# Two pieces of GpSimd's work placed behind a block's sums: sketched attention followed by an exact-GELU MLP

## Chip, cores and metric

The kernel runs on one core of a Trainium2 chip. The metric is device time in microseconds; times given are medians over runs, and a separate profiled execution gives the trace. The engines are called TensorE (PE in the profile; PEld is its weight load), VectorE (DVE), ScalarE (ACT), GpSimd (POOL) and SyncE (SP, which here only issues transfers).

## What is computed

Attention with a polynomial sketch in place of the softmax, and behind it an MLP of two matmuls with an exact GELU between them:

```python
def phi(x):                                   # S1, S2: 8 x 32
    a = np.einsum('rd,bhsd->bhsr', S1, x)
    b = np.einsum('rd,bhsd->bhsr', S2, x)
    return np.einsum('bhsi,bhsj->bhsij', a, b).reshape(*x.shape[:-1], 64)
q_p, k_p = phi(q), phi(k)                     # q, k, v: 4 x 4 x 1088 x 32
kv = np.einsum('bhsf,bhsd->bhfd', k_p, v)
z = np.sum(k_p, axis=2)
num = np.einsum('bhsf,bhfd->bhsd', q_p, kv)
den = np.einsum('bhsf,bhf->bhs', q_p, z)[..., None] + 1e-06
x = (num / den).transpose(0, 2, 1, 3).reshape(4352, 128)
h = x @ w_in                                  # 128 x 2048
out = (0.5 * h * (1 + erf(h / sqrt(2)))) @ w_out   # 2048 x 128
```

w_in, w_out, S1 and S2 come as 64-bit floats, so the kernel forms 32-bit floats from their words on the chip.

## The kernel before

**Tiling.** The 1088 tokens of each of the four batches are two chunks of 512 and a remainder of 64. The eight chunks of 512 are n = 0 to 7, and the remainders of all batches together are the last one. For each chunk the 2048 hidden channels are 16 tiles of 128, so a step t is one pair of a chunk and a hidden tile. Steps 0 to 3 are tiles 0 to 3 of chunk 0, steps 4 to 11 tiles 0 to 7 of chunk 1, steps 12 to 23 the rest of chunk 0, steps 24 to 31 the rest of chunk 1, and from step 32 on each chunk has its 16 steps in a row.

**Order.** Each engine executes its instructions in the order of the text: the last lines of the kernel tie every instruction to the one before it on its engine. The text is the loop at L1289. In each step it first issues the hidden tile's matmul and GELU (`hidden`, L770 and L777), then, in every fourth step, the sums of the block that this tile completes (`token_sums`), then the entries that `at(t, function, arguments)` put in the list of that step, in the order in which they were entered, then stores and then products on TensorE that are due. So the step and the place in the list set where a piece of work stands in an engine's queue.

**The second matmul.** The first tiles of chunks 0 and 1 (4 and 8 of them) are multiplied by w_out as usual (`project`, L955). All others go in blocks of four hidden tiles, by a scheme with seven products in place of eight. A block needs sums of its activations, which GpSimd makes in `token_sums` (L821 to L824; they are called bits_low, bits_a, bits_e and bits_m in the profile, after the buffers that they share with the rounding), and sums of quarters of w_out, which GpSimd makes once for each piece of w_out in `channel_sums` (L808 to L811, into tiles called small). w_in and w_out are each five pieces: 0 to 4. The products are issued by `two_products` (L856) some steps behind the block's last tile. The blocks in question are, in chunk 0, the first (its last tile is step 15), the second (step 19) and the third (step 23); the second uses piece 3 of w_out and the third piece 4.

**Rounding.** Pieces 2 to 4 of w_in and w_out are formed in steps 4 to 13 by VectorE and ScalarE, in the order of the list `turns`. On VectorE, `end` issues the mantissa (L302), the sign (L307) and the product (L312). For `turns[4]`, which is piece 4 of w_in, GpSimd does the product: `multiply`, in step 12.

**The keys of the second batch (batch 1).** In steps 13 to 18 VectorE turns and multiplies its keys (L383, L1082 to L1104) and the next queries (L556), and in step 24 TensorE sums keys and values (`z_sum`, `kv_and_attend`, both by way of L456), after which VectorE folds z (L511 to L514) for TensorE's sketch of the queries (L606). For the 64 remaining tokens the values lie in `v_rem_aug`, a tile that GpSimd clears (L364) and into which it copies the 64 rows (L366) that a transfer brought; this is `widen_v_rem(1)`. The transfer is one of many that SyncE issues in a row.

**GpSimd's queue from step 12 to 23**: `widen_v_rem(1)`, `multiply` of w_in's piece 4, `channel_sums(2)` (step 13), the sums of the first block (step 15), `channel_sums(3)` (16), `channel_sums(4)` (18), the sums of the second block (19) and those of the third (23).

Of the kernel before, what the change touches and what calls it, by code (L numbers as in the profile page):

```python
# [16 lines left out]
def kernel(  # L17
# [1046 lines left out]
    def at(t, f, *a):  # L1064
        slots[t].append(lambda: f(*a))
# [112 lines left out]
    for k, acts in enumerate(schedule):  # L1178
# [4 lines left out]
            at(t, by_scalar, turns[k], *what)  # L1183
        if k + 1 < len(turns):
            at(t1, end, turns[k])
    at(12, widen_v_rem, 1)
    at(12, multiply, turns[4])
    for i, t in ((1, 5), (0, 6), (2, 13)):
        at(t, channel_sums, i)
    at(16, channel_sums, 3)  # L1190
# [6 lines left out]
    at(17, features_rem, 1)  # L1197
    at(17, add_tokens, 1)
    at(18, query_turn, 2)
    at(18, channel_sums, 4)  # L1200

    at(24, z_sum, 1)
    at(24, fold_z, 1)
# [181 lines left out]
```

## Time and profile before

| | |
|---|---|
| time before | 257.99 us median of 3 runs (257.95 to 258.36) |
| profiled execution | 259.27 us, its span 257.5 us |
| TensorE clock granted | 0.999 |
| busy in the span | TensorE 252.0, VectorE 159.5, ScalarE 113.6, GpSimd 176.8 us |
| read from HBM, written | 10.88 MB, 2.23 MB |

The span is the stretch from the first to the last instruction of the trace, and all places in the trace are counted in us from its start. The profiled execution is one single run with the profiler on; its own time, not the median, belongs to its span. In a row of the timeline the bracket gives the idle time of the engine ahead of the instruction, and what ended it. Such a releaser is inferred from semaphore events.

### The profile page before, as it was taken

Reading aid. Unit: us, or ns where it says so; the run is one execution under the profiler, and the core shown is the slowest. Engines: PE = TensorE matmul, PEld = TensorE weight load, DVE = VectorE, ACT = ScalarE, POOL = GpSimd, SP = SyncE. Lnnn points to the kernel's source line nnn. Section 1 sums busy time; section 2 is a strip of 40 time slices with the busy share of each in tenths; the row PEclk is TensorE's granted clock in tenths of the full one; section 3 lists DMA queues with packets and bytes.
Section 4 is the critical chain, followed back from the end, with each engine's and each line's share of the span. In section 5 each row is a group of like instructions: output and inputs, shape, how many; then the busy total and the mean of one; then the engine's idle time right before and its main releaser. Section 6 shows DMA issues by size and latency. Waiting matters only on the chain.

```text
span 257.5 us, 5987 instructions
## 1 busy us (share of the span) xinstructions
PE 252.0 (98%) x2421; PEld 131.2 (51%) x2421; DVE 159.5 (62%) x334; ACT 113.6 (44%) x219; POOL 176.8 (69%) x193
## 2 busy tenths in 40 slices
PE   8999999989999999999999999999999999999995
PEld 4744444455444545544444455455544444445784
DVE  4899999929799997590187986399407000700282
ACT  3783885323626333443335332533435333532541
POOL 3517219998858778487758775687758777877950
PEclk9999999999999999999999999999999999999999
DMA  6789538821000101102000002000110200020021
GB/s 209 209 257 305 147 71 222 210 64 15 0 3 12 29 4 19 25 1 42 0 3 0 0 7 38 1 4 0 26 17 3 42 0 3 4 36 3 0 35 32
DMA packets 29083, 13.50 MB, mean 52 GB/s; under 512 B 21888, under 2 KB 27264, under 8 KB 29056
## 3 DMA queue, kind: packets, MB, share of 16 engines
q1 hardware_dynamic: 28624, 12.79, 20.5%
q8 instruction: 19, 0.31, 0.6%
q10 hardware_dynamic: 432, 0.33, 0.4%
q14 instruction: 8, 0.07, 0.1%
HBM read 10.88 MB, written 2.23 MB: 51 GB/s over the span
## 4 chain that ended last, share of the span: by engine, by line
PE 81%; DMA 6%; POOL 6%; SPq 4%; ACT 1%; issue 1%; DVE 0%; POOLq 0%
PE h_ps L770 38%; PE o_ps L856 33%; DMA block<-in_moe_w_out_dram 6%; PE w_ps L926 2%; SPq L125 2%; PE w_ps L456 1%; PE w_ps L606 1%; PE w_ps L661 1%; PE w_ps L987 1%; POOL bits_low L821 1%; DMA v_rem<-in_v_dram 1%; SPq L181 1%; PE o_ps L952 1%; POOL small L811 1%; POOL bits_m L824 0%
## 5 line engine op out<-in xcount | busy, mean ns | idle before, releaser
L770 PE MATMUL h_ps<-xT,w_in 128*64 128x512 f32 (+2 forms) x536 | 137.9, 567 | 0.0
L777 ACT ACTIVATE block<-h_ps 128x512 f32<-128x512 f32 (+1 forms) x132 | 75.4, 572 | 121.1 <-PE h_ps L770 119.1
L856 PE MATMUL o_ps<-block,w_out 128*64 128x256 f32 x232 | 59.5, 379 | 0.0
L821 POOL TENSOR_TENSOR bits_low<-block 128x512 f32<-128x512 f32 x29 | 38.0, 1311 | 28.9 <-ACT block L777 28.9
L770 PEld LDWEIGHTS h_ps<-xT,w_in 128*64 128x64 f32 (+1 forms) x536 | 41.4, 140 | 27.1 <-issue 8.2
L856 PEld LDWEIGHTS o_ps<-block,w_out 128*64 128x64 f32 x232 | 31.7, 137 | 38.6 <-issue 27.7
L822 POOL TENSOR_TENSOR bits_a<-block 128x512 f32<-128x512 f32 x29 | 37.0, 1277 | 12.3 <-ACT block L777 12.3
L871 DVE COPY sums<-o_ps 64x256 f32<-64x256 f32 x8 | 3.3, 416 | 60.2 <-PE o_ps L856 60.2
L823 POOL TENSOR_TENSOR bits_e<-bits_a,block 128x512 f32<-128x512 f32 x29 | 37.3, 1288 | 2.3
L824 POOL TENSOR_TENSOR bits_m<-block,bits_e 128x512 f32<-128x512 f32 x29 | 37.0, 1277 | 2.3
L856 PE MATMUL o_ps<-bits_low,small 128*64 128x256 f32 x116 | 29.9, 380 | 1.3 <-POOL bits_low L821 1.3
L856 PE MATMUL o_ps<-block,small 128*64 128x256 f32 x116 | 30.0, 380 | 0.0
L856 PE MATMUL o_ps<-bits_m,w_out 128*64 128x256 f32 x116 | 29.8, 379 | 0.0
L856 PE MATMUL o_ps<-bits_a,small 128*64 128x256 f32 x116 | 29.8, 379 | 0.0
L856 PEld LDWEIGHTS o_ps<-block,small 128*64 128x64 f32 x116 | 15.6, 137 | 18.5 <-issue 11.1
L856 PE MATMUL o_ps<-bits_e,small 128*64 128x256 f32 x116 | 17.7, 383 | 0.0
L856 PEld LDWEIGHTS o_ps<-bits_low,small 128*64 128x64 f32 x116 | 15.6, 137 | 1.9 <-POOL bits_low L821 1.8
L856 PEld LDWEIGHTS o_ps<-bits_a,small 128*64 128x64 f32 x116 | 15.8, 137 | 0.5 <-POOL bits_a L822 0.3
L856 PEld LDWEIGHTS o_ps<-bits_m,w_out 128*64 128x64 f32 x116 | 15.9, 137 | 0.0
L618 DVE STREAM_TRANSPOSE w_ps<-w_ps 128x512 f32<-128x512 f32 (+1 forms) x7 | 4.8, 687 | 17.1 <-ACT xT L672 12.7
L856 PEld LDWEIGHTS o_ps<-bits_e,small 128*64 128x64 f32 x116 | 7.8, 136 | 11.5 <-issue 9.0
L955 PE MATMUL o_ps<-g,w_out 128*128 128x512 f32 x24 | 12.1, 600 | 0.1
(221 smaller groups left out, 317.7 us busy)
## 6 DMA issues: line engine op xcount, KB each, us to landing
block<-in_moe_w_in_dram SPq DMA_DIRECT2D x3, 512.0 KB, 13.0
block<-in_moe_w_out_dram SPq DMA_DIRECT2D x3, 512.0 KB, 12.8
k<-in_k_dram SPq DMA_DIRECT2D x12, 128.0 KB, 2.8
v<-in_v_dram SPq DMA_DIRECT2D x12, 128.0 KB, 2.8
q<-in_q_dram SPq DMA_DIRECT2D x24, 64.0 KB, 2.4
out_dram<-oT SPq DMA_DIRECT2D x21, 64.0 KB, 2.3
q_first<-in_q_dram SPq DMA_DIRECT2D x2, 256.0 KB, 3.9
v<-in_v_dram SPq DMA_DIRECT2D x2, 256.0 KB, 4.2
```

The costliest lines, as they stand in the source:

```text
L125: sp.dma_start(out=q_sb[n][h * 32:(h + 1) * 32].rearrange("t x j d -> t (x j d)"), in_=q[n // NCH, h, at:at + CW, :].rearrange("(t n) d -> ...
L618: dve.transpose(out=tok, in_=ps[:, :, :H2])
L770: pe.matmul(ps[rows, :W], lhsT=w[:, rows], rhs=xT[n][:, :W], start=True, stop=True)
L777: act.activation(out=g_of[n, fi][:, :W], in_=ps[:, :W], func=ACT.Gelu)
L821: pool.tensor_sub(out=s[3], in0=a11, in1=a21)
L822: pool.tensor_add(out=s[1], in0=a21, in1=a22)
L823: pool.tensor_sub(out=s[2], in0=s[1], in1=a11)
L824: pool.tensor_sub(out=s[4], in0=a12, in1=s[2])
L856: pe.matmul(acc[n][bank][half * 64:(half + 1) * 64, col:col + HW], lhsT=fixed, rhs=moving, start=opens and e == 0 and name in "4715", stop ...
L871: dve.tensor_copy(out=N[lo, 0, one], in_=a0[lo, one])
L926: pe.matmul(acc[NMAIN][rows, COLS_REM[name]], lhsT=tokens[:, rows], rhs=fixed, start=k == 0 and name == ORDER_REM[0], stop=k == BLOCKED // ...
L955: pe.matmul(o_of[n][:, cols], lhsT=w_tile(w_out_sb, fi), rhs=g[:, cols], start=first, stop=final)
```

## The change

Two entries of the list go to other steps. `widen_v_rem(1)` goes from step 12, where it stood ahead of `multiply`, to step 15, where it follows the sums of the first block. `channel_sums(4)` goes from step 18 to step 19, where it follows the sums of the second block. No instruction is added or left out.

```diff
-    at(12, widen_v_rem, 1)
     at(12, multiply, turns[4])
+    at(15, widen_v_rem, 1)
     for i, t in ((1, 5), (0, 6), (2, 13)):
         at(t, channel_sums, i)
     at(16, channel_sums, 3)
...
     at(18, query_turn, 2)
-    at(18, channel_sums, 4)
+    at(19, channel_sums, 4)
```

GpSimd's queue after it: `multiply` (step 12), `channel_sums(2)` (13), the sums of the first block and `widen_v_rem(1)` (15), `channel_sums(3)` (16), the sums of the second block and `channel_sums(4)` (19), the sums of the third block (23).

## The prediction

> **What bounds the kernel now.** The page's busy times come first: TensorE is busy for 252.0 of 257.5 us.
>
> ```profile
> PE 252.0 (98%) x2421; PEld 131.2 (51%) x2421; DVE 159.5 (62%) x334; ACT 113.6 (44%) x219; POOL 176.8 (69%) x193
> ```
>
> So a gain can only come from the few places where TensorE stands still. The view of waits (engine, line, releaser: us in total, times, longest us) shows one wait of TensorE's matmuls on GpSimd, and one long wait of GpSimd on a transfer:
>
> ```profile
> POOL v_rem_aug L366 <- DMA v_rem<-in_v_dram: 10.5, 1, 10.5
> ...
> PE o_ps L856 <- POOL bits_low L821: 1.3, 1, 1.3
> ```
>
> The chain that ended last, in order of time, joins the two (start us, us, what):
>
> ```profile
> 35.23 2.30 DMA v_rem<-in_v_dram
> ...
> 37.65 0.75 POOL v_rem_aug L366
> 38.40 1.26 POOL w_in L312
> ...
> 50.50 0.46 POOL small L811
> 50.95 1.24 POOL bits_low L821
> 52.19 0.04 issue
> 52.23 0.86 PE o_ps L856 x5
> ...
> 55.89 1.25 PE w_ps L456 x80
> ```
>
> The transfer of the remainder's values lands at 37.53. GpSimd then copies it (L366), multiplies w_in's last piece (L312), and works without a pause until the first of the second block's sums (bits_low, L821) ends at 52.19. From 52.23 on the chain is TensorE alone but for the output's last step. Both things that the change moves lie in that run.
>
> The stall's true size is read from the timeline (start us, us, instruction), against an undisturbed stretch with the same order (two steps of products and hidden matmuls, then L456):
>
> ```profile
> 50.30 0.59 PE L856 MATMUL o_ps<-block,small 128*64 128x256 f32 x2
> 52.23 0.43 PE L856 MATMUL o_ps<-bits_low,small 128*64 128x256 f32 x1 [1.33 <-POOL bits_low L821]
> ...
> 55.82 0.32 PE L456 MATMUL w_ps<-k_s,ones 128*32 128x64 f32 x8
> ...
> 94.14 0.38 PE L856 MATMUL o_ps<-block,small 128*64 128x256 f32 x1
> ...
> 97.68 0.32 PE L456 MATMUL w_ps<-k_s,ones 128*32 128x64 f32 x8
> ```
>
> Undisturbed it takes 97.68 - 94.14 = 3.54 us from these products to L456; here 55.82 - 50.30 = 5.52. The stall costs 1.98 us, more than the 1.33 in its row, because the products that don't need bits_low ran ahead and stood idle after. Ahead of 50.30 and behind 55.82 I see no other stall that GpSimd causes and TensorE pays for.
>
> **The copy (step 12 to 15).** L364 and L366 leave the place ahead of L312. The cleared tile needs no data, but the copy holds all that is behind it in GpSimd's queue until 37.53. L312 then waits only for VectorE's sign step of the same piece, which ends at 35.77 + 0.68 = 36.45:
>
> ```profile
> 35.77 0.68 DVE L307 SCALAR_TENSOR_TENSOR bits_e<-block,bits_r 128x512 uint32<-128x512 uint32 x1
> ...
> 38.17 3.27 DVE L307 SCALAR_TENSOR_TENSOR bits_e<-block,bits_r 128x512 uint32<-128x512 uint32 x1
> 40.97 0.79 POOL L811 TENSOR_TENSOR small<-w_out,small 128x128 f32<-128x128 f32 x1
> 41.72 1.72 POOL L821 TENSOR_TENSOR bits_low<-block 128x512 f32<-128x512 f32 x1
> ...
> 88.02 0.20 POOL L364 MEMSET v_rem_aug<- 128x128 f32 x1
> 88.29 0.29 POOL L366 COPY v_rem_aug<-v_rem 64x128 f32<-64x128 f32 x1
> ```
>
> With the 0.04 us that a release takes here (52.19 to 52.23) L312 starts at 36.49 in place of 38.36: 1.87 us sooner. Its input and the channel sums behind it are ready by then (w_out's piece 2 was written by 29.4). The first block's bits_low needs the GELU of step 14 (37.83 + 0.62 = 38.45), its second sum that of step 15 (39.45 + 0.60 = 40.05); GpSimd reaches them at 36.49 + 1.25 + 1.82 = 39.6 and 40.8, so neither wait shows. The clearing and the copy come back behind the block's four sums, on the path now: 0.56 us by the later rows above (88.02 to 88.58), 0.48 + 0.75 = 1.23 by the rows at 26.70 and 37.65. I take 0.56, since the 0.75 met VectorE's L302 and the reduction that VectorE runs at 46 shows no such effect on the sums beside it. The transfer has then long landed. Who needs the copy is kv_sum at 56.85 - 1.98 = 54.9; it is ready before 47.
>
> **The channel sums of the last piece (step 18 to 19).** They took 49.13 to 50.91, 1.78 us, directly ahead of bits_low of the second block; that goes. They come behind that block's sums: their first reader is the third block's products at 61.00 - 1.98 = 59.0.
>
> **The sum.** L312's start to the end of bits_low was 52.19 - 38.36 = 13.83. Less 1.78, plus 0.56: 12.61 (13.28 with the dear copy). Started at 36.49 it ends at 49.10 (49.77). One thing is added: VectorE's last rounding (L302, L307, L312) falls on the same stretch. Before, two of its three steps held GpSimd up, L811 by 0.34 and L821 by 0.44 us against their sister rows, which is in the 13.83; now L302 (37.60) falls on it too. I take one more such delay, 0.45: 49.55, at the worst 50.22. Below, if fewer collide than before, 48.3. The second block's GELUs are done by 45.52. TensorE wants bits_low at 50.30. **The stall goes whole, 1.98 us, with 0.08 to 2 us to spare.**
>
> What is late next: the second block's next sum, bits_a, ends 1.24 us behind bits_low, at 50.8 (51.5 at the worst), and is wanted two steps of 0.86 behind 50.30, at 52.0; its last sum ends 3.87 us behind, at 53.4, and is wanted at 59.06 - 1.98 = 57.1; the last channel sums at 55.2, wanted at 59.0; the third block's bits_low at 56.5, wanted at 59.0, its last sum at 60.4, wanted at 65.73 - 1.98 = 63.75. On VectorE, k_s (L1104) ends at 50.95 and L456 wants it at 53.84; L556 ends at 52.16 and z's step (L511) would start at 54.23. All hold. Behind them the whole order follows TensorE, and no load is outstanding past 62 us that is wanted soon, so 1.98 us reach the end.
>
> The Trainium skill (SBUF — State Buffer, Who interferes with whom) states that a VectorE instruction with two SBUF inputs and a GpSimd one that reads SBUF exclude each other, the later one blocked until the first finishes. The trace agrees that they collide, but the 3.27 row ran across four GpSimd instructions, not one. By the page each of the three steps would get in after one instruction and hold GpSimd for its own 0.68 us: estimated from rows, 3 x 0.68 - 0.78 = 1.26 in place of 0.45, bits_low at 50.36, and a loss of 0.06 us.
>
> **The time.** Profiled execution 259.27 us (span 257.5 and 1.77 around it): 259.27 - 1.98 = 257.29. The median of the runs shown, 257.99, lies 1.28 lower; on it I forecast **256.0 us**. Repeated runs lie within 257.95 to 258.36, so about 0.2% (0.52 us) can be told from no change.
>
> **Rivals.**
> (a) GpSimd is still late in part: all three VectorE steps hold it for their whole 0.68 us and the copy costs 1.23: 36.49 + 13.28 + 1.26 = 51.03, a stall of 0.73, time 256.7. For it: the collisions at 38 to 43. Against: no GpSimd row there lost over 0.46.
> (b) VectorE is late. GpSimd now runs from 36.49 with gaps only where an instruction needs the one before it (the 0.07 us ahead of L811, and between the later sums). If each rounding step waits for a gap of its own: 39.0, 42.4, 44.3, the rounding ends at 44.9 in place of 42.30, 2.6 us late; L556 then ends at 54.8, 0.5 past 54.23, and TensorE's sketches wait some 0.4 us: time 256.4.
> (c) Slower: the same mechanism, but VectorE is let in only when the first block's sums and the copy are over, at about 45.2. Three steps of 0.65 end at 47.1, 4.8 late; 2.1 of it is covered, so TensorE stands 2.7 us at the sketches ahead of L606 and the time is 257.99 - 1.98 + 2.7 = 258.7. It turns slower from a lateness of about 4.1 us. Against: the 3.27 row was let in at the gap of 40.90.
> (d) No change: the stall returns at the second block's next sum or at the third block. Against: the margins above of 1.2 us and more (0.5 at the worst). 258.0.
>
> **Chances.** Forecast 0.76 (255.7 to 256.3), (a) 0.06, (b) 0.06, (c) 0.07, (d) 0.05. (a) and (b) are still faster by over 0.2%: faster 0.88, same 0.05, slower 0.07. The range takes in the forecast's spread and (a) and (b): 255.5 to 256.9.
>
> **What would show it.** In the changed profile: L312 on GpSimd near 36.5; the wait of 10.5 us under L366 gone; L366 at about 45 to 46 and about 0.3 us long; bits_low of the second block ending at 48.3 to 50.2; no row of L856 waiting on bits_low; L456 near 53.8 with nothing ahead of it; the chain on TensorE all through that stretch. I am wrong if L312 on VectorE ends past 44.5, if L511 starts later than 0.4 us behind L456, or if bits_low ends past 50.3.

## The result and the profile after

The changed kernel takes 257.75 us (median of 22 runs, 257.29 to 258.15). The kernel before, run beside it, takes 258.57 us (22 runs, 257.95 to 259.94). The ratio is 0.9968, with a 95% interval of 0.9957 to 0.9978: faster by 0.82 us, 0.3%, where 2.0 us were forecast. The 256.0 us of the forecast lie below every run of the changed kernel.

The profiled execution of the changed kernel took 257.70 us, its span 255.9. First the page: TensorE's busy time, and the chain that ended last, by engine.

```profile
PE 251.6 (98%) x2421; PEld 131.2 (51%) x2421; DVE 157.5 (62%) x334; ACT 113.6 (44%) x219; POOL 177.3 (69%) x193
...
PE 98%; ACT 0%; DVE 0%; issue 0%
```

In the kernel before, transfers (6%), GpSimd (6%) and SyncE's queue (4%) held about a sixth of that chain, which went back from the stall through GpSimd's wait to the loads ahead of it; now it is TensorE from end to end. The timeline of the place in question, GpSimd first and TensorE second (start us, us, instruction, and in brackets what the engine waited for):

```profile
36.91 1.31 POOL L312 TENSOR_TENSOR w_in<-bits_m,bits_e 128x512 f32<-128x512 f32 x1 [9.71 <-DVE bits_e L307]
38.16 0.92 POOL L808 TENSOR_TENSOR small<-w_out 128x128 f32<-128x128 f32 x1
...
46.74 0.29 POOL L366 COPY v_rem_aug<-v_rem 64x128 f32<-64x128 f32 x1
...
48.77 1.28 POOL L821 TENSOR_TENSOR bits_low<-block 128x512 f32<-128x512 f32 x1
```

```profile
50.73 0.38 PE L856 MATMUL o_ps<-block,small 128*64 128x256 f32 x1
50.74 0.38 PE L856 MATMUL o_ps<-bits_low,small 128*64 128x256 f32 x1
...
54.27 0.32 PE L456 MATMUL w_ps<-k_s,ones 128*32 128x64 f32 x8
```

GpSimd's product (L312) waits for VectorE alone, the copy takes 0.29 us behind the first block's sums, and bits_low of the second block ends at 50.05, ahead of the products that read it. These now take 54.27 - 50.73 = 3.54 us to L456, the undisturbed figure to the hundredth. The stall is gone whole. So the question is why a stall of 1.98 us that went whole brought 0.82.

Two differences between the two profiles point to the answer. The first products of the second block begin at 50.73 now and began at 50.30 then. Of these 0.43 us, 0.38 are there already ahead of the place where the copy stood: VectorE's sign step (L307), for which GpSimd's product waits, ends at 36.83 now and ended at 36.45 then. And SyncE issued the three transfers among which is the one that the copy waits for from 31.67 on in this execution, from 35.23 on in the one before. Nothing in the order of SyncE's queue was changed, so this may vary from one execution to the next.

**Theory A**: the profiled execution of before was not a usual one. The values land usually before VectorE releases L312, so that L312 starts late only in a few executions, and the stall is usually some 0.6 to 0.7 us; what causes it there is the channel sums ahead of bits_low. **Theory B**: the landing delays GpSimd in a usual execution too, the stall is near 2 us, and the change has a cost of about 1.1 us elsewhere.

### The profile page after: what moved, and what is told of

It reads as the page before. It is cut to its first block, busy times and chain, and to the rows that moved or that the text cites. A ratio compares the mean times of both kernels' runs of the same rounds, so it can differ in the third digit from the quotient of the medians.

```text
span 255.9 us, 5988 instructions
## 1 busy us (share of the span) xinstructions
PE 251.6 (98%) x2421; PEld 131.2 (51%) x2421; DVE 157.5 (62%) x334; ACT 113.6 (44%) x219; POOL 177.3 (69%) x193
## 4 chain that ended last, share of the span: by engine, by line
PE 98%; ACT 0%; DVE 0%; issue 0%
PE h_ps L770 45%; PE o_ps L856 35%; PE o_ps L955 4%; PE w_ps L926 2%; PE w_ps L456 1%; PE w_ps L606 1%; PE w_ps L661 1%; PE w_ps L987 1%; PE w_ps L572 1%; PE h_ps L786 1%; PE o_ps L952 1%; PE h_ps L348 1%; PE o_ps L445 1%; PE w_ps L1074 1%; PE w_ps L681 0%; PE o_ps L397 0%
## 5 line engine op out<-in xcount | busy, mean ns | idle before, releaser
L821 POOL TENSOR_TENSOR bits_low<-block 128x512 f32<-128x512 f32 x29 | 37.5, 1292 | 28.2 <-ACT block L777 28.2
L770 PEld LDWEIGHTS h_ps<-xT,w_in 128*64 128x64 f32 (+1 forms) x536 | 40.8, 140 | 27.1 <-issue 8.2
L822 POOL TENSOR_TENSOR bits_a<-block 128x512 f32<-128x512 f32 x29 | 37.1, 1280 | 11.6 <-ACT block L777 11.5
L823 POOL TENSOR_TENSOR bits_e<-bits_a,block 128x512 f32<-128x512 f32 x29 | 37.4, 1289 | 2.3
L856 PEld LDWEIGHTS o_ps<-bits_e,small 128*64 128x64 f32 x116 | 7.9, 137 | 11.5 <-issue 9.1
## 6 DMA issues: line engine op xcount, KB each, us to landing
q_first<-in_q_dram SPq DMA_DIRECT2D x2, 256.0 KB, 3.9
v<-in_v_dram SPq DMA_DIRECT2D x2, 256.0 KB, 4.1
```

The source lines that it names most:

```text
L770: pe.matmul(ps[rows, :W], lhsT=w[:, rows], rhs=xT[n][:, :W], start=True, stop=True)
L821: pool.tensor_sub(out=s[3], in0=a11, in1=a21)
L822: pool.tensor_add(out=s[1], in0=a21, in1=a22)
L823: pool.tensor_sub(out=s[2], in0=s[1], in1=a11)
L856: pe.matmul(acc[n][bank][half * 64:(half + 1) * 64, col:col + HW], lhsT=fixed, rhs=moving, start=opens and e == 0 and name in "4715", stop ...
```

## The experiments

In all of them the comparison is with the kernel before, run on the same chip.

### The halves of the change, an early transfer, and the change again

The copy alone:

```diff
-    at(12, widen_v_rem, 1)
     at(12, multiply, turns[4])
+    at(15, widen_v_rem, 1)
```

> Only the copy is moved (step 12 to 15); the channel sums of the last piece stay ahead of the second block's sums. Theory A (in a usual execution the remainder's values land early, so that GpSimd's w_in product waits for VectorE in the kernel before too; what makes bits_low of the second block late is the work ahead of it): in the profile after, bits_low ended at 50.05 and was wanted at 50.73; 1.78 us of channel sums put it at 51.83, 1.1 us late, a stall of about 1.2, and a time 1.2 us above the changed kernel's, that is 0.4 us ABOVE the kernel before. Theory B (the landing holds the w_in product up in a usual execution too, so the move is worth 1.3 us at the path, and the change carries a cost of about 1.1 us elsewhere): 0.2 to 1.3 us BELOW the kernel before.

Measured: 258.96 us (11 runs) against 258.55, ratio 1.0019 (1.0010 to 1.0029): slower by 0.4 us, as theory A had it to a tenth. TensorE's timeline has a stall of 55.68 - 50.98 - 3.54 = 1.16 us:

```profile
50.98 0.59 PE L856 MATMUL o_ps<-block,small 128*64 128x256 f32 x2
52.09 0.43 PE L856 MATMUL o_ps<-bits_low,small 128*64 128x256 f32 x1 [0.52 <-POOL bits_low L821]
...
55.68 0.32 PE L456 MATMUL w_ps<-k_s,ones 128*32 128x64 f32 x8
```

The half that takes the 10.5 us wait out of the view of waits makes the kernel slower: GpSimd's product now waits 9.72 us for VectorE in its place, and the copy, which stood in idle time, stands on the path.

The channel sums alone:

```diff
-    at(18, channel_sums, 4)
+    at(19, channel_sums, 4)
```

> Only the channel sums of the last piece are moved (step 18 to 19); the copy stays ahead of the w_in product. Theory A: no stall in a usual execution, since 1.78 us go and at most 0.6 were late; the time is the changed kernel's within 0.1 us, 0.8 us below the kernel before. A late landing (37.5) would leave a stall of about 0.1 to 0.2 only. Theory B: 1.78 of the 1.98 us go here, less a hidden cost if this half carries it: anything from 0.7 to 1.8 us below the kernel before, and slower than the changed kernel by 0.1 to 0.3.

Measured: 257.57 us (9 runs), ratio 0.9971 (0.9961 to 0.9982), against 257.69 for the whole change in the same comparison; the ratios of the two, 0.9971 and 0.9968, can't be told apart. This half brings all of the gain. In its profile the values land early, bits_low ends at 48.02 + 1.27 = 49.29, and the products take 54.12 - 50.58 = 3.54 us to L456:

```profile
48.02 1.27 POOL L821 TENSOR_TENSOR bits_low<-block 128x512 f32<-128x512 f32 x1
...
50.58 0.38 PE L856 MATMUL o_ps<-block,small 128*64 128x256 f32 x1
...
54.12 0.32 PE L456 MATMUL w_ps<-k_s,ones 128*32 128x64 f32 x8
```

A gain of this size was also within theory B's range, so this run doesn't decide between the two.

The order as before, with the transfer ahead of the loads of batch 1:

```diff
+        load_rem("v", 1)
         for b in range(1, B):
             load_keys(b)
...
-                for n, b1 in (("k", 1), ("k", 3), ("v", 1), ("v", 2), ("v", 3)):
+                for n, b1 in (("k", 1), ("k", 3), ("v", 2), ("v", 3)):
```

> The order on GpSimd as before; only the transfer of the remainder's second values is issued ahead of the keys and values of batch 1, some 6 us sooner, so that the copy finds them there. Theory A: nothing changes in the usual execution: a stall of 0.6 to 0.7 us remains, bits_low of the second block ends about 0.6 us past the time it is wanted, L312 on GpSimd starts on VectorE's L307; the median is 0 to 0.2 us below the kernel before, with fewer high times. Theory B: L312 starts 1.9 us sooner, the stall goes nearly whole: 1.5 to 1.9 us below the kernel before.

Measured: 258.33 us (12 runs, 257.99 to 258.90), ratio 0.9996 (0.9986 to 1.0006): no difference that can be told. The transfer was issued at 15.22, 15 to 21 us sooner than in the profiles that leave it in its place, and not the 6 us of the expectation, so the landing is out of the way altogether (line numbers are one higher in this kernel), and yet:

```profile
27.42 0.35 POOL L367 COPY v_rem_aug<-v_rem 64x128 f32<-64x128 f32 x1
36.81 1.31 POOL L313 TENSOR_TENSOR w_in<-bits_m,bits_e 128x512 f32<-128x512 f32 x1 [9.04 <-DVE bits_e L308]
...
49.92 1.27 POOL L822 TENSOR_TENSOR bits_low<-block 128x512 f32<-128x512 f32 x1
```

GpSimd idles 9 us all the same, now for VectorE, and bits_low ends at 51.19 where the products stand ready from 50.47; they take 4.37 us to L457, a stall of 0.83, a little more than theory A's 0.6 to 0.7. Theory B, which wanted 1.5 to 1.9 us of gain, falls here.

The changed kernel once more:

> The changed kernel itself, beside its halves on one chip, and with a second profile. Theory A: 0.7 to 0.9 us below the kernel before; TensorE without a stall up to the sums of keys and values; the start of the first long matmuls varies by some 0.4 us between profiles, in stretches that the change doesn't touch. Theory B: the same time, with a place that is longer by about 1 us than in the kernel before in each profile.

Measured: 257.69 us (11 runs), ratio 0.9968 (0.9957 to 0.9979). Its second profile (258.07 us) has the products at 51.00 and L456 at 54.54, again 3.54 us. From L456 to the end of the span it takes 256.2 - 54.54 = 201.7 us, as the kernel before did (257.5 - 55.82 = 201.7): theory B's hidden cost isn't there. Ahead of the products, 51.00 lies within the kernel before's own scatter (50.30 to 51.03, next section).

### The kernel before, three more profiles

> The kernel before, a second profile. Theory A: the landing of the remainder's second values differs from profile to profile by several us (33 to 38); where it lies ahead of VectorE's L307 (about 36.5 to 37) L312 on GpSimd waits for that L307 and the stall ahead of bits_low is 0.6 to 0.7 us of time (from the first products of the second block to L456: 4.1 to 4.3 us in place of 5.52). Theory B: the landing comes past 37 and the stall is near 2 us again.

> The kernel before, a third profile, for the scatter: as in the second. If the landing is late again, theory A wants a longer stall and a time above the median to go with it.

> The kernel before once more, for the scatter of the landing against the stall: start of the first products of the second block between 50.3 and 51.0; a landing past 37 with a stall of 1.5 to 2 us, one ahead of 36 with 0.6 to 0.8 us; the time is the start of these products plus 3.54 plus the stall plus 201.7 of span.

| execution of the kernel before | time, us | copy starts, just behind the landing | L312 on GpSimd starts | first products | bits_low ends | stall |
|---|---|---|---|---|---|---|
| the one of the prediction | 259.27 | 37.65 | 38.36 | 50.30 | 52.18 | 1.98 |
| again | 259.74 | 38.08 | 38.33 | 50.99 | 52.58 | 1.69 |
| third | 258.30 | 33.75 | 36.76 | 50.63 | 51.14 | 0.61 |
| fourth | 258.87 | 35.70 | 37.38 | 51.03 | 51.79 | 0.85 |

The stall is the time from the first products to L456, less 3.54. In all four it is bits_low's lateness behind the first products, and 0.1 us. The sum that was expected of the fourth holds: 51.03 + 3.54 + 0.85 + 201.7 = 257.1, which is its span, and in the three others and in both profiles of the changed kernel it comes out within 0.1 us. So the start of these products and the stall are all that the spans differ by. Of the 22 runs of the kernel before, four took over 259.1 us, where the two late profiles lie; that the landing was late in just these is likely, but not shown.

What makes the landing late was not tried, but the pages of the profiles show something that goes along with it. The three 512 KB transfers of w_out, which stand earlier in SyncE's queue, took 10.0 us to land (median of the three) in the third profile, 11.5 in the fourth, and 12.8 and 13.1 in the two late ones, in the order of the landings.

The third profile, which is near the median, in the order GpSimd, TensorE:

```profile
33.75 0.47 POOL L366 COPY v_rem_aug<-v_rem 64x128 f32<-64x128 f32 x1 [5.93 <-DMA v_rem<-in_v_dram]
36.76 1.30 POOL L312 TENSOR_TENSOR w_in<-bits_m,bits_e 128x512 f32<-128x512 f32 x1 [2.54 <-DVE bits_e L307]
...
49.86 1.28 POOL L821 TENSOR_TENSOR bits_low<-block 128x512 f32<-128x512 f32 x1
```

```profile
50.63 0.59 PE L856 MATMUL o_ps<-block,small 128*64 128x256 f32 x2
51.20 0.43 PE L856 MATMUL o_ps<-bits_low,small 128*64 128x256 f32 x1
...
54.78 0.32 PE L456 MATMUL w_ps<-k_s,ones 128*32 128x64 f32 x8
```

The wait for the transfer ends at 33.75 and a second wait follows, for VectorE, which the profile of the prediction did not have. A wait can be long and yet end before the next one does.

### A late transfer

The transfer goes behind the values of batch 2, in the kernel before, in the changed one, and in the one with the channel sums moved alone:

```diff
             load_values(b)
+            if b == 2:
+                load_rem("v", 1)
             for c in range(NCH):
                 load_q(b * NCH + c)
...
-                for n, b1 in (("k", 1), ("k", 3), ("v", 1), ("v", 2), ("v", 3)):
+                for n, b1 in (("k", 1), ("k", 3), ("v", 2), ("v", 3)):
```

> The kernel before with the transfer of the remainder's second values issued some 4 us later, behind batch 2's values. Theory A: the landing now sets L312 in each execution; landing at 38.5 to 41, bits_low some 14.6 us later, so a stall of 2.5 to 5 us: 260.3 to 262.8. Theory B: the same direction and about the kernel before plus 4 us: 262 to 263.

> The changed kernel with the same late transfer. Both theories: the copy stands at about 46.5 on GpSimd and finds the values there (landing at 38.5 to 41): no stall, the time of the changed kernel within 0.2 us. If it is slower, the later transfers that are displaced matter, and the run before is spoiled by that.

> The late transfer again (issued behind batch 2's values), with only the channel sums moved and the copy still ahead of the w_in product: what is the move of the copy worth when the landing is late? In the late kernel before, bits_low ended 2.16 us past the first products (53.40 against 51.24); less 1.78 it is 0.4 late in an execution like that one, and from 0 to 1.9 in others, since that kernel ran from 260.3 to 262.9 us. Theory A: 258.0 to 259.6, between the late changed kernel (257.69) and the late kernel before (261.41), by 1.8 to 2.1 us below the latter. Theory B, by which the landing is what matters: within 1 us of the late kernel before.

Measured: 261.41 us in the order of before (260.31 to 262.89; ratio 1.0127, 1.0074 to 1.0180), 257.69 in the changed one (0.9966, 0.9956 to 0.9976), 260.06 with the channel sums moved alone (1.0065, 1.0048 to 1.0082). The first two medians came as expected, though the stall in the first one's profile, 57.04 - 51.24 - 3.54 = 2.26, is less than the 2.5 us of theory A. The third missed its range of 258.0 to 259.6: I had counted the second block's products only. In its profile the copy starts at 41.38, so late that the first block's sums are late too (line numbers are two higher here):

```profile
45.33 0.59 PE L858 MATMUL o_ps<-block,small 128*64 128x256 f32 x2
45.99 0.43 PE L858 MATMUL o_ps<-bits_low,small 128*64 128x256 f32 x1
...
48.57 0.65 PE L858 MATMUL o_ps<-bits_e,small 128*64 128x256 f32 x4 [0.65 <-POOL bits_e L825]
```

TensorE waits for bits_low and for bits_e of the first block before it comes to the second, whose products begin at 52.50 and have a stall of 56.53 - 52.50 - 3.54 = 0.49 besides. So the move of the copy does protect against a late landing, by 260.06 - 257.69 = 2.4 us here (on two chips, on which the kernel before took 258.48 and 258.63). With the transfer where it was, the copy started between 33.60 and 38.08 in the five profiles in which it stood ahead of L312, never so late as here.

## Why the prediction was wrong

**The stall, 1.98 us: rightly read, wrongly carried over.** The term that was mis-sized is the stall of the execution that the median stands for. The prediction took 1.98 us from one profiled execution, noted that this execution lay 1.28 us above the median, and subtracted the whole stall from the median all the same. What these 1.28 us were is known now. The median was that of three runs; 22 runs have 258.57, so 0.58 are three runs that happened to be low. The other 0.70 are what this execution's stall had beyond the usual one, less its early start of the products (below). The usual stall is 0.6 to 0.9 us (third and fourth profile, and the early transfer's), and the gain of 0.82 agrees with that. The forecast lay 1.74 us too low: 0.58 by the median and 1.98 - 0.82 = 1.16 by the stall. Taken from its own execution, the sum is not bad: 259.27 - 1.98 = 257.29 is the fastest of the 22 runs of the changed kernel, as an execution with the earliest start and no stall should be.

**Where the products begin.** That same execution had the earliest start of these products, 50.30, against 50.47 to 51.03 in the nine other profiles that have no stall ahead of them. In all ten they begin 13.7 to 14.0 us behind the end of VectorE's L307. So where the landing is early and L312 waits for L307, GpSimd moves along with TensorE and the stall stays what it is (0.61, 0.85, 0.83). Where the landing is late, GpSimd doesn't move along, and an early TensorE lengthens the stall; the profile had both. Without a stall the difference stays in the time: the changed kernel's two profiles have 50.73 and 51.00, and their spans are 255.9 and 256.2.

**The copy, "1.87 us sooner": wrong for the usual execution.** L312 starts between 36.7 and 37.4 with the landing early, in the kernel before too. The wait for the landing had ended before another, that for L307, did. The move takes nothing off the path there and puts the copy on it: the copy alone costs 0.4 us. In the whole change this cost is covered by the 0.68 us to spare (below). The size of the copy (0.56 forecast; 46.46 to 46.99 measured, 0.53) was right.

**The channel sums, 1.78 us: right.** They are what removes the usual stall: alone they bring the whole gain. By the sum, any lateness of bits_low below 1.78 us goes with them; no run with a lateness between 0.8 and 1.78 us was made to show that.

**The collisions with VectorE: right in size, on other instructions.** Three were forecast, 0.34 us on L811, 0.44 on L821 and 0.45 more, 1.23 in all. L808, L809 and L810 took 0.92, 0.90 and 0.90 us in place of 0.45, 1.37 in all, and L811 and L821 lost nothing. The steps got in after one instruction each, which the prediction had worked out beside its forecast; but each held GpSimd for some 0.45 us, not for the 0.68 taken there. L312's start to the end of bits_low was forecast at 13.06 us and measured at 50.05 - 36.91 = 13.14. The margin was 0.68 us (50.73 - 50.05), within the forecast one.

**The rivals.** (a) did not come: bits_low ended 0.68 us ahead of the products. (b) did not come either: VectorE's last rounding ended at 39.66 + 0.83 = 40.49, earlier than before, and L511 followed L456 by 54.66 - 54.27 = 0.39. (c) fell with that. (d), no change, was nearer to the size than the forecast, though for no reason that it gave. The rival that was missing is the one that came true: that the profiled execution shows more of the stall than the median contains.

## What to carry to other kernels

When a stall is read from one profiled execution, compare that execution's time with the median first, and with a median of more than three runs: what lies between them may be part of the stall, and a forecast for the median can't subtract more than a typical execution has. Ask of a wait that ends on a transfer what would be waited for if the transfer came 2 us sooner; where another release lies right behind it, only the work that is always on the path (here four channel sums) is worth moving. A move of idle-time work onto the path takes its length, from the slack or from the time, in every execution, and pays only in those where its wait was the last to end.

## What the runs showed of the hardware

**How long VectorE stands when it collides with GpSimd** was not the same with an early and with a late landing, and I had taken it from one row. In the kernel before, with the landing late, a rounding step with two inputs in SBUF stood through GpSimd's next four instructions (the second profile, VectorE first and then GpSimd):

```profile
38.27 3.14 DVE L302 SCALAR_TENSOR_TENSOR bits_m<-bits_a,bits_low 128x512 f32<-128x512 uint32 x1
```

```profile
38.33 1.29 POOL L312 TENSOR_TENSOR w_in<-bits_m,bits_e 128x512 f32<-128x512 f32 x1
...
40.94 0.79 POOL L811 TENSOR_TENSOR small<-w_out,small 128x128 f32<-128x128 f32 x1
```

Where L312 on GpSimd had waited for VectorE, the same three steps took turns with GpSimd's channel sums, one instruction against one: VectorE's took 0.80, 0.94 and 0.83 us in the changed kernel, GpSimd's 0.92, 0.90 and 0.90, against about 0.68 and 0.45 undisturbed:

```profile
37.97 0.80 DVE L302 SCALAR_TENSOR_TENSOR bits_m<-bits_a,bits_low 128x512 f32<-128x512 uint32 x1
38.69 0.94 DVE L307 SCALAR_TENSOR_TENSOR bits_e<-block,bits_r 128x512 uint32<-128x512 uint32 x1
39.66 0.83 DVE L312 TENSOR_TENSOR w_out<-bits_m,bits_e 128x512 f32<-128x512 f32 x1
```

The Trainium skill (SBUF — State Buffer, Who interferes with whom) states that the later of two such instructions is blocked until the first finishes. The taking of turns agrees with that; the steps of 3.14 and 3.27 us, which stood through four, do not. In both late profiles the long step began while GpSimd was at the copy (38.27 against 38.08 to 38.36, 38.17 against 37.65 to 38.40), in the others VectorE's L302 began during GpSimd's L312; what decides between the two was not tried.

**A late start of GpSimd can be partly paid back.** From L312's start to the end of bits_low the order of before takes 51.14 - 36.76 = 14.38 us with the landing early (third profile), 52.18 - 38.36 = 13.82 and 52.58 - 38.33 = 14.25 in the two late ones, and 53.40 - 40.38 = 13.02 in the late transfer's profile, where VectorE's rounding was over by then (it ended at 39.57 + 0.69 = 40.26, and GpSimd's product began at 40.38). The 1.36 us between the first and the last are the three collisions, 3 x 0.45.
